# A one-core decode block: the load of w2's blocks 6 to 9 in transfers of 112, 9 and 7 partitions, and the wait for the result's store behind the section

## The chip, the cores and the metric

The kernel runs on one core of a Trainium2 chip. The metric is the device time of one execution in microseconds (us), lower is better. The time before is the median of three runs. A further execution was recorded by the hardware profiler; its rows are what this document reads.

## The reference

One decode step of a transformer layer for four sequences, one token each, in bfloat16: layer norm, attention over a cache of 4096 keys and values for 32 heads, and a dense layer with the activation h * tanh(softplus(h)).

```python
x = A_x                                   # [4, 1, 640]
q = (layernorm(x) @ A_wq)                 # [4, 32 heads, 1, 128]
p = softmax(q . k_cache * 128 ** -0.5)    # k_cache [4, 32, 4096, 128]
h = x + (p @ v_cache) @ A_wo              # v_cache [4, 32, 4096, 128]
u = layernorm(h) @ B_w1 + B_b1            # B_w1 [640, 1728]
h2 = h + (u * tanh(softplus(u))) @ B_w2   # B_w2 [1728, 640]
```

The two caches are 134 MB each; everything is read once.

## The kernel before

**Attention.** The work is cut into 16 units (four groups of eight heads for each of four sequences). A unit's keys or values are one transfer of 128 partitions by 65536 bytes, into one of three slots of SBUF. For a unit VectorE multiplies the keys by the broadcast query in the slot (line 628), TensorE sums over the head dimension with an identity matrix (L640), VectorE reduces (L615), a softmax follows (L677 to L725), and TensorE multiplies with the values (L750). The loads are issued on SP's queue long ahead; a slot is loaded again when its last reader is done.

**The tail.** After the last units the freed slots take the weights of the rest, each with its own transfers, all issued from SP by the helper `load` (its `dma_start` is L867): two halves of wo, three parts of w1, then w2 into slot `wend2`. w2 has 13 whole blocks of 128 rows and a rest of 64 rows, which is loaded alone (L892) into partitions 64 to 127. The boundaries of the transfers of the 13 blocks stand in `W2P`; the first 12 blocks lie two rows to a partition, so that one packet holds 2560 bytes:

```python
W2P = (0, 6, 10, 12, C2)      # C2 = 13: blocks 0-5, 6-9, 10-11, 12
w2_view = B_w2[0 : C2E * 128, :].rearrange("(m p k) n -> p m (k n)", p=128, k=2)
```

The transfer of blocks 6 to 9 is 128 partitions by two packets of 2560 bytes, 640 KB; that of blocks 10 and 11 is 128 by one packet, that of block 12 is 128 by one packet of 1280 bytes, and it is the last load of the kernel.

TensorE then projects with wo (L966), the second layer norm follows (L1007 to L1060), the products with w1 (L1032), the activation on VectorE and ScalarE (L1070 to L1091), and the products with w2 (`w2_products`, L1118). These go in the order of the loads: the rest of 64 rows, then the transfers in order, each group waiting for its transfer's semaphore (w2_0, w2_6, w2_10, w2_12) and for the activation. VectorE and ScalarE copy the four partial rows out of PSUM (`gather`, L1134), and SP stores 4 x 640 values (L1143).

**Who orders it.** The instructions are not scheduled by the framework. A small recorder, the class `Program`, takes every operation with the names that it reads and writes (`P.add`, and `do` for the tail), works out the semaphore waits, and writes each engine's instructions in order, the loop over the units included. A transfer adds 16 to its semaphore when all of it has landed; each transfer has a semaphore named after it. `P.emit()` runs inside `tc.tile_critical()`, one section for the framework, and the section ends with SP's wait for the store's semaphore:

```python
with tc.tile_critical():
    P.emit()
    nc.sync.wait_ge(P.sems["out"], P.totals["out"])
```

Behind the section the framework writes its own closing steps: a handshake of SP with the other engines for the section (the profile gives it the line of the `with`, L1148), and then the closing barrier of the kernel (L1176).

Of the kernel before, what the change touches and what calls it, by code (L numbers as in the profile page):

```python
# [223 lines left out]
def kernel(  # L224
# [13 lines left out]
    nc = tc.nc  # L238

    B, Sq, D = A_x.shape  # L240
# [31 lines left out]
    W2P = (0, 6, 10, 12, C2)  # L272
# [21 lines left out]
    S_BANK, TR, QQ, OB, OT = [("bank", i) for i in range(4)], *[("bank", i) for i in range(4, 8)]  # L294
# [40 lines left out]
    P = Program(nc, tc, 1, NU - 1, NS)  # L335
# [4 lines left out]
    def cells(i, lo=0, hi=SLOT):  # L340

        return [("slot", i, p, k) for p in range(lo // PART, -(-hi // PART)) for k in range(NQ)]
# [5 lines left out]
    def load_kv(what, rows, u, i, parts=1):  # L348
        w = SLOT // parts
        for k in range(parts):  # L350
# [41 lines left out]
            out=ident[:, :],  # L392
# [27 lines left out]
    def bn_stats():  # L420
        for s in range(2):
# [13 lines left out]
            out=ln_std[:, :], in_=ln_mv[:, 1:2], func=ACT.Sqrt, bias=eps_t[0:N, :], scale=1.0  # L435
# [13 lines left out]
            out=ln1_bf,  # L449
# [40 lines left out]
    def identity_sums(dst, pattern, name, **kw):  # L490
# [13 lines left out]
            out=own[:, :], in0=own1[:, :], scalar1=-1.0, scalar2=1e30, op0=ALU.add, op1=ALU.mult  # L504
# [27 lines left out]
    def q_all():  # L532
        for h in range(H):
# [15 lines left out]
            out=qT[:, 0 : NU * G].rearrange("p (o b g) -> p b o g", o=NO, b=N),  # L549
# [273 lines left out]
    def slot_of(u):  # L823
        return 1 if u == 0 else 2 * u % NS
# [21 lines left out]
    i1, i2, i3 = slot_of(NU - 1), slot_of(NU - 2), slot_of(NU - 3)  # L846
# [11 lines left out]
    def load(out_ap, in_ap, i, lo, hi, name, sem=None):  # L858


        ops = {}
        for cell in cells(i, lo, hi):
            for d in P.readers.get(cell, {}).values():
                ops[d.nth] = d
        P.add(
            "SP",
            lambda: nc.sync.dma_start(out=out_ap, in_=in_ap),  # L867
            w=[name],
            sem=sem or "_".join(map(str, name)),
            after=ops.values(),  # L870
        )
# [3 lines left out]
    for k0, k1 in zip(W1P, W1P[1:]):  # L875
# [17 lines left out]
        w=["w2r"],  # L893
        sem=f"slot{i2}",
    )
    for k0, k1 in zip(W2P, W2P[1:]):
        if k0 < C2E:
            assert k0 % 2 == k1 % 2 == 0
            to = wend2[:, k0 * D : k1 * D].rearrange("p (m n) -> p m n", n=2 * D)
            of = w2_view[:, k0 // 2 : k1 // 2]  # L900
        else:
            to, of = w2_sb[:, k0, :], B_w2[k0 * 128 : k1 * 128, :]
        load(to, of, i2, k0 * D, k1 * D, ("w2", k0))

    at = [nw2]

    def scratch(n, dt=FP32):
        a = at[0]
        w = n * (2 if dt == FP32 else 1)
        w += w % 2  # L910
        at[0] = a + w
        ap = wend2[:, a : a + w]
        return ap.bitcast(FP32)[:, 0:n] if dt == FP32 else ap[:, 0:n]

    def do(eng, emit, r=(), w=()):

        return P.add(eng, emit, r=r, w=w, after=[last_pv])
# [123 lines left out]
    for dc in range(DC):  # L1041
        w1 = ("w1", max(k0 for k0 in W1P if k0 <= dc))
        do("PE", lambda dc=dc: h1_pass(dc), [w1, "h2T"], [QQ])
        if dc == 1:
# [4 lines left out]
                    out=std, in_=v_ps, func=ACT.Sqrt, bias=eps_t[:, :], scale=1.0  # L1049
# [22 lines left out]
    def stt(out_, a, scalar, b, op0, op1, r, w):  # L1072
# [13 lines left out]
            out=tc_, in0=tb, scalar1=-0.5, scalar2=-1.0, op0=ALU.mult, op1=ALU.add  # L1086
# [27 lines left out]
    def w2_products(blocks):  # L1114
        for c in blocks:
            w2 = w2_sb[:, c, :] if c < C2 else w2r_sb
            for t in range(OT4):
                ins = nc.tensor.matmul(  # L1118
                    y2[32 * t : 32 * t + N, :],
                    lhsT=act_t[:, c, :],  # L1120
                    rhs=w2[:, t * DT : (t + 1) * DT],
                    start=False,
                    stop=(c == C2 - 1),
                )
        return ins
# [1 line left out]
    do("PE", residual, ["hT", "ident_f"], [S_BANK[1]])  # L1127
    do("PE", lambda: w2_products([C2]), ["w2r", "act"], [S_BANK[1]])
    for k0, k1 in zip(W2P, W2P[1:]):
        do("PE", lambda b=range(k0, k1): w2_products(b), [("w2", k0), "act"], [S_BANK[1]])  # L1130
    out_bf = scratch(D, BF16)[0:N, :]

    def gather(t, copy):
# [11 lines left out]
        sem="out",  # L1145
    )

    with tc.tile_critical():  # L1148
        P.emit()
        nc.sync.wait_ge(P.sems["out"], P.totals["out"])  # L1150


# [28 lines left out]
```

## Time and profile before

| | us |
|---|---|
| median of three runs | 666.3 (666.23 to 666.72) |
| profiled execution, its own time | 666.91 |
| its span, first to last instruction | 665.1 |
| TensorE busy in the span | 378.2 (57%) |
| VectorE busy | 352.4 (53%) |
| ScalarE busy | 89.1 (13%) |
| read from HBM | 283.35 MB, 426 GB/s over the span |
| mean granted TensorE clock | 0.821 |

The profile's page gives busy time by engine, 40 equal slices of the span, the DMA queues (q1 is SP's), the chain of work that ended last, and groups of equal instructions with their source line (L). PE is TensorE's matmul, PEld its weight load, DVE VectorE, ACT ScalarE, POOL GpSimd, SP the sync engine; SPq stands for SP's own instructions, those that issue DMAs among them. Times in the span count from its first instruction. Beside the page the trace was asked for stretches of the span, for single lines, for waits, and read packet by packet at the end of the load.

### The profile page before, as it was taken

What the parts mean: (1) busy time and instruction counts of PE and PEld (TensorE: products, weight loads), DVE (VectorE), ACT (ScalarE), POOL (GpSimd) and SP (SyncE); (2) the same over time, 40 slices, a digit from 0 to 9 for tenths busy, and PEclk for the clock granted to TensorE, in tenths of its full rate; (3) what the DMA queues carried; (4) which work ended last, traced back from release to release, by engine and by line L of the source; (5) the groups of instructions that cost most, each with busy time, mean ns of one, the idle gap of its engine ahead of it and who ended that gap; (6) DMA issues with size and microseconds to landing.
All of it is one profiled execution on the core that took longest, in us unless ns stands there. A gap on an engine that the chain in (4) does not pass through costs nothing.

```text
span 665.1 us, 6908 instructions
## 1 busy us (share of the span) xinstructions
PE 378.2 (57%) x2803; PEld 173.3 (26%) x2803; DVE 352.4 (53%) x313; ACT 89.1 (13%) x318; POOL 2.4 (0%) x12
## 2 busy tenths in 40 slices
PE   0355768375482837548283754828375582837765
PEld 0221323132130313213031322303132230313334
DVE  2065869184472818447390835738093573809402
ACT  0102020202002020200202020020202002020211
POOL 1000000000000000000000000000000000000000
PEclk9999799779596978959697895969788596978865
DMA  9999999999999999999999999999999999999996
GB/s 379 438 441 435 441 388 442 438 437 427 434 434 426 430 437 441 434 430 437 434 422 434 437 441 434 430 434 430 430 430 441 437 430 437 434 430 430 420 417 253
DMA packets 6685, 283.52 MB, mean 426 GB/s; under 512 B 713, under 2 KB 913, under 8 KB 2066
## 3 DMA queue, kind: packets, MB, share of 16 engines
q1 hardware_dynamic: 6664, 283.35, 99.0%
q8 instruction: 8, 0.13, 0.1%
q14 instruction: 3, 0.02, 0.0%
q10 hardware_dynamic: 10, 0.01, 0.0%
HBM read 283.35 MB, written 0.01 MB: 426 GB/s over the span
## 4 chain that ended last, share of the span: by engine, by line
DMA 44%; DVE 25%; PE 19%; another core or an unknown queue 6%; issue 2%; SPq 2%; ACT 1%; DVEq 0%; POOL 0%; ACTq 0%
DMA slot<-in_A_k_cache_dram 41%; DVE slot L628 21%; PE bank L640 13%; PE bank L750 5%; DMA slot<-in_B_w_dram 3%; DVE s_sb L615 3%; SPq L867 2%; ACT e L725 1%; PE bank L708 0%; DVE mx L695 0%; PE bank L686 0%; DVE rl L802 0%; DVE otn L809 0%; DVEq L217 0%
## 5 line engine op out<-in xcount | busy, mean ns | idle before, releaser
L640 PE MATMUL bank<-slot,ident 128*128 128x512 bf16 x1024 | 271.1, 419 | 246.1 <-DVE slot L628 246.1
L628 DVE TENSOR_TENSOR slot<-slot,qb 128x4096 bf16<-128x4096 bf16 x128 | 288.3, 2284 | 156.3 <-DMA slot<-in_A_k_cache_dram 151.9
L640 PEld LDWEIGHTS bank<-slot,ident 128*128 128x128 bf16 x1024 | 100.6, 106 | 401.8 <-DVE slot L628 278.8
L615 DVE TENSOR_REDUCE s_sb<-bank 128x64 f32<-128x512 f32 x64 | 44.0, 688 | 55.7 <-PE bank L640 55.7
L725 ACT ACTIVATE e<-s_sb,nb 128x256 bf16<-128x256 f32 x128 | 63.1, 494 | 46.9 <-DVE nb L717 46.9
L750 PE MATMUL bank<-slot,e 128*32 128x512 bf16 x1024 | 61.2, 393 | 5.2 <-DMA slot<-in_A_v_cache_dram 3.4
L595 ACT CAST qb<-bank 128x128 bf16<-128x128 f32 x17 | 4.5, 265 | 306.1 <-PE bank L586 306.1
L750 PEld LDWEIGHTS bank<-slot,e 128*32 128x32 bf16 x1024 | 26.4, 99 | 38.1 <-issue 8.7
L770 ACT COPY o_sb<-bank 128x512 f32<-128x512 f32 x16 | 9.4, 585 | 183.6 <-PE bank L750 183.6
L695 DVE TENSOR_REDUCE mx<-bank 1x8 f32<-1x128 f32 x16 | 4.5, 279 | 39.9 <-PE bank L686 39.9
L725 ACT ACTIVATION_READ_ACCUMULATOR e<-s_sb,nb 128x1 f32 x128 | 23.9, 187 | 0.0
L783 PE MATMUL bank<-sel,o_sb 128*128 128x8 f32 x136 | 18.5, 262 | 0.0
L783 PEld LDWEIGHTS bank<-sel,o_sb 128*128 128x128 f32 x136 | 17.4, 200 | 0.0
L802 DVE RECIPROCAL rl<-bank 128x8 f32<-128x8 f32 x17 | 3.4, 202 | 15.6 <-PE bank L783 15.6
L535 PE MATMUL bank<-xT,slot 128*128 128x4 bf16 x160 | 4.4, 168 | 10.8 <-DMA slot<-in_A_wq_dram 10.8
L708 PE MATMUL bank<-mx,nscale 1*128 1x8 f32 x32 | 6.1, 262 | 5.9 <-DVE mx L695 5.9
L569 DVE COPY b1T<-bank 128x14 f32<-128x14 f32 x1 | 0.2, 173 | 14.2 <-PE bank L559 14.2
L781 PEld LDWEIGHTS bank<-rs,ones_f 128*128 128x128 f32 x34 | 6.5, 197 | 3.8 <-ACT o_sb L770 1.6
L708 PEld LDWEIGHTS bank<-mx,nscale 1*128 1x128 f32 x32 | 4.7, 183 | 10.6 <-DVE mx L695 10.6
L535 PEld LDWEIGHTS bank<-xT,slot 128*128 128x128 bf16 x160 | 4.3, 104 | 10.9 <-DMA slot<-in_A_wq_dram 10.9
L677 DVE TENSOR_REDUCE pm<-s_sb 128x1 f32<-128x256 f32 x16 | 6.7, 420 | 0.5
L686 PE MATMUL bank<-ident_f,pm 128*1 128x128 f32 x32 | 6.1, 272 | 1.2 <-DVE pm L677 1.2
(75 smaller groups left out, 67.6 us busy)
## 6 DMA issues: line engine op xcount, KB each, us to landing
slot<-in_A_v_cache_dram SPq DMA_DIRECT2D x2, 4096.0 KB, 45.3
slot<-in_A_wq_dram SPq DMA_DIRECT2D x1, 5120.0 KB, 15.3
slot<-in_A_wo_dram SPq DMA_DIRECT2D x2, 2560.0 KB, 33.6
slot<-in_B_w_dram SPq DMA_DIRECT2D x2, 864.0 KB, 34.0
slot<-in_B_w_dram SPq DMA_DIRECT2D x1, 960.0 KB, 31.9
slot<-in_B_w_dram SPq DMA_DIRECT2D x1, 640.0 KB, 32.9
slot<-in_B_w_dram SPq DMA_DIRECT2D x1, 432.0 KB, 33.7
slot<-in_B_w_dram SPq DMA_DIRECT2D x1, 320.0 KB, 22.5
```

Source lines behind the costliest of these rows:

```text
L535: ins = nc.tensor.matmul(qT_ps[:, :, h], lhsT=wq_sb[:, c, h * Dh : (h + 1) * Dh], rhs=xT[:, c, :], start=(c == 0), stop=(c == DC - 1),)
L615: lambda: nc.vector.tensor_reduce(out=s_sb[:, part * RP : (part + 1) * RP], in_=s_bank[part][:, :].rearrange("p (r w) -> p r w", w=W), axi ...
L628: return nc.vector.tensor_tensor(out=kt, in0=kt, in1=qbs[u % NS][:, k * DQ : (k + 1) * DQ] .unsqueeze(1) .to_broadcast([128, RP, DQ]), op= ...
L640: ins = nc.tensor.matmul(s_bank[part][:, :].rearrange("p (r w) -> p r w", w=W), lhsT=ident[:, :], rhs=kt[:, :, d : d + W], start=(d == 0), ...
L677: lambda: nc.vector.tensor_reduce(out=pm[:, :], in_=s_sb[:, :], axis=AX.X, op=ALU.max),
L708: lambda: nc.tensor.matmul(nb_ps, lhsT=nscale[:, :], rhs=mx[:, :], start=True, stop=True),
L725: ins = nc.scalar.activation(out=e2[:, :, h, :], in_=s_sb[:, :].rearrange("p (g r) -> p g r", r=RQ), func=ACT.Exp, bias=nb[:, h : h + 1], ...
L750: ins = nc.tensor.matmul(o_bank[t : t + G * RQ, :], lhsT=e2[:, g, :, :], rhs=vt[:, g * RQ : (g + 1) * RQ, :], start=(g < CT), stop=(g >= N ...
L770: lambda: nc.scalar.copy(out=o_sb[:, :], in_=o_bank[:, :]),
L781: nc.tensor.matmul(l_ps, lhsT=ones_f[:, :], rhs=rss[u % NS][:, :], start=True, stop=True)
L783: ins = nc.tensor.matmul(o_ps, lhsT=o_sb[:, r * Dh : (r + 1) * Dh], rhs=sel[:, r, :], start=(r == 0), stop=(r == RQ - 1),)
L867: lambda: nc.sync.dma_start(out=out_ap, in_=in_ap),
```

## The change

Two edits. First, the load of blocks 6 to 9 is cut by partitions, 0 to 111, 112 to 120 and 121 to 127, into three transfers, issued one after the other; the other w2 transfers stay whole. The three share the semaphore w2_6, and the products of these blocks wait for all of them. Second, SP's wait for the store is taken out of the section and written behind it, with the count in a register and a declared dependence on the section.

```diff
+    w2_parts = {}
     for k0, k1 in zip(W2P, W2P[1:]):
...
-        load(to, of, i2, k0 * D, k1 * D, ("w2", k0))
+
+        cuts = (0, 112, 121, 128) if k0 == W2P[1] else (0, 128)
+        for p0, p1 in zip(cuts, cuts[1:]):
+            load(to[p0:p1], of[p0:p1], i2, k0 * D, k1 * D, ("w2", k0, p0), f"w2_{k0}")
+        w2_parts[k0] = [("w2", k0, p0) for p0 in cuts[:-1]]
...
-        do("PE", lambda b=range(k0, k1): w2_products(b), [("w2", k0), "act"], [S_BANK[1]])
+        do("PE", lambda b=range(k0, k1): w2_products(b), [*w2_parts[k0], "act"], [S_BANK[1]])
...
-    with tc.tile_critical():
+    with tc.tile_critical() as section:
         P.emit()
-        nc.sync.wait_ge(P.sems["out"], P.totals["out"])
+
+    wait = nc.sync.wait_ge(P.sems["out"], nc.sync.to_reg(P.totals["out"]))
+    tc.add_manual_dep(
+        wait.ins,
+        section.name,
+        mybir.DependencyInfo(mybir.DependencyClass.NoSync, mybir.DependencyReason.DATA),
+        reason="the store is issued in the section",
+    )
```

In the built program the engines' other instructions stand in the same order as before; on SP two DMA instructions are added, and its wait for the store stands in the handshake behind the section, after the drain and before the last step.

## The prediction

> **What bounds the kernel now.** I read the page first, then the last microseconds by stretches, then what the last matmuls and SP's last instructions wait for.
>
> From the page: span, DMA slices, and the queues with their packets.
>
> ```profile
> span 665.1 us, 6908 instructions
> ...
> DMA  9999999999999999999999999999999999999996
> ...
> q1 hardware_dynamic: 6664, 283.35, 99.0%
> ...
> q10 hardware_dynamic: 10, 0.01, 0.0%
> ```
>
> The 16 DMA engines are over 90% busy in every slice but the last. 283.35 MB must come in, and only what happens in or after the last slice can end earlier by rearrangement. Both edits lie there. The profiled execution took 666.91 us, 1.79 us more than its span; the median of the runs shown is 666.3, 0.6 below it. I work out differences on the profiled one and take them from the median.
>
> The end of the load, in stretches (columns: stretch, its length, busy time of PE, PEld, DVE, ACT, POOL, granted clock, share of the 16 DMA engines that is busy, GB/s):
>
> ```profile
> 655.00:658.50 3.50, 2.06 (x59) 1.62 (x56) 1.74 (x7) 1.88 (x4) 0.00 (x0) 0.50 1.04 370
> 658.50:659.00 0.50, 0.49 (x18) 0.50 (x21) 0.00 (x0) 0.00 (x0) 0.00 (x0) 0.50 0.94 351
> 659.00:659.50 0.50, 0.50 (x20) 0.27 (x8) 0.00 (x0) 0.00 (x0) 0.00 (x0) 0.50 0.79 284
> 659.50:660.00 0.50, 0.11 (x4) 0.00 (x0) 0.00 (x0) 0.00 (x0) 0.00 (x0) 0.50 0.59 220
> 660.00:660.50 0.50, 0.42 (x16) 0.36 (x16) 0.00 (x0) 0.00 (x0) 0.00 (x0) 0.50 0.28 102
> 660.50:661.00 0.50, 0.38 (x18) 0.09 (x8) 0.00 (x0) 0.00 (x0) 0.00 (x0) 0.50 0.09 31
> 661.00:662.00 1.00, 0.64 (x12) 0.10 (x7) 0.31 (x1) 0.30 (x2) 0.00 (x0) 0.50 0.00 0
> ```
>
> The engines don't finish together: the share falls from 0.94 to 0.09 over two microseconds. The trace's packet records say it exactly: the packets of the last transfer (block 12 of w2) are through on the first engine at 658.87 us and on the last two at 660.81 and 660.82; the next before these is 0.2 us earlier. All engines were given equal bytes, so this is the lag that each carries from earlier, not its share.
>
> From the timeline, the last products, the copies out and the store:
>
> ```profile
> 660.08 1.55 PE L1118 MATMUL bank<-slot 128*4 128x160 bf16 x28 [0.47 <-DMA slot<-in_B_w_dram]
> ...
> 661.33 0.09 PEld L1118 LDWEIGHTS bank<-slot 128*4 128x4 bf16 x4 [0.32 <-DMA slot<-in_B_w_dram]
> 661.69 0.58 ACT L1134 CAST slot<-bank 4x160 bf16<-4x160 f32 x2 [4.59 <-PE bank L1118]
> 661.69 0.65 DVE L1134 CAST slot<-bank 4x160 bf16<-4x160 f32 x2 [3.33 <-PE bank L1118]
> 662.37 0.35 SPq L1143 DMA_DIRECT2D out_dram<-slot  x1
> ```
>
> PE waits for the load at 660.08, 660.91 and 661.33, the last time for w2_12. So the slowest DMA engine sets the end, followed by one chain of products, copies, store and closing steps.
>
> What stands between the store's landing and the span's end (instructions of lines 1148 and 1176; duration min/median/max in ns, first and last start), and SP's wait:
>
> ```profile
> L1148 SPq EVENT_SEMAPHORE  x3: 17/28/28, 663.9 to 664.1; - x3
> L1148 SPq COMPARE_BRANCH  x1: 38/38/38, 663.7 to 663.7; - x1
> L1176 SPq DRAIN  x3: 7/7/7, 664.3 to 664.6; - x3
> SPq L1148 <- DMA out_dram<-slot: 1.0, 1, 1.0
> ```
>
> The store lands at 663.70. Only then does SP run the closing handshake of the section (line 1148: an event, the other engines' drains, two more events and a NOP), and only then the kernel's own closing barrier (line 1176).
>
> **The wait moved behind the section.** It removes the wait from SP's branch and puts it into the handshake. In the built program SP, after issuing the store, branches without waiting, sends its event, drains, and waits in three events: for PE, for DVE and ACT, and third for itself and the store together; then come the NOP and the drains of line 1176. One register move is added, before the wait.
>
> Read singly in the trace of before: wait ends 663.706, event 663.879, drain 663.976, events 664.055 and 664.119, NOP 664.186, line-1176 drains 664.272 and 664.335. After: the third event starts with the landing (663.706 as the branch did), and from there the same steps as before hold: event to NOP 0.067, NOP to drain 0.086, drain to drain 0.063, so the second drain stands at 663.922 instead of 664.335. That is **-0.41 us**. What now hides the earlier handshake is the store's flight: SP's issue ends at 662.72 and the landing is 1.0 us later, while the moved steps (event to second event, 0.24, and the step from branch to event, 0.17) take 0.41, and the register move some 0.05, the step of SP's other small instructions. Without that cover it would cost its 0.41 again. Queued behind the waiting event on SP are only the NOP and the drains; the other four engines have by then passed line 1148 and wait in line 1176's barrier, as before. POOL's closing events, 664.4 to 665.0, follow SP's drain and shift with it.
>
> **Blocks 6 to 9 in three transfers.** Bytes are the same, 640 KB. Two DMA instructions and their semaphore writes are added, nothing else; PE's wait is for 48 instead of 16 on the same semaphore, at 660.08, not the last wait.
>
> SP's side: an issue that finds room takes 0.33 to 0.58 us; two of the last ones are longer:
>
> ```profile
> 627.12 11.17 SPq L867 DMA_DIRECT2D slot<-in_B_w_dram  x1
> 638.33 9.14 SPq L867 DMA_DIRECT2D slot<-in_B_w_dram  x1
> ```
>
> These block because the queue is full, so they end when the DMA engines get on, not after a price of their own. The last load's issue ends at 649.26 and its first packet runs at 658.44 on the fastest engine: 9.2 us of cover. Two issues at 0.58 and up to four more queued packets on an engine, at 0.27 us (the 6912-byte packets running then), come to 1.2 + 1.1 = 2.3 us. I take **0**; the bound above is two more blocked issues (rival below), and nothing is gained, since SP is ahead anyway.
>
> The engines' side: a 128-row transfer gives each engine 8 rows of two 2560-byte packets. The 112 rows give 7 each. For the rest the nearest row is q10: ten packets for a 4-row and a 1-row transfer, that is one data packet per row and one semaphore packet for each of four engines and one engine. So I take one row per engine for the 9 and for the 7. Together engines then carry 7 to 9 rows instead of 8. A row costs 5120 bytes at 370 GB/s / 16, or 0.22 us (2 packets at their median of 0.108 in the trace, the same). So the last engine ends **between -0.22 and +0.24** (a row plus two semaphore packets of about 0.01): down if both late engines get fewer rows, up if either gets one more. The trace doesn't name the engines of its packets, so it can't decide; I take **0** and keep both ends. The engines that end third and earlier leave 0.2 us, so relief cannot exceed about that unless they are relieved too.
>
> [...]
>
> **Sum:** -0.41 + 0 + 0 = -0.41, so 666.3 - 0.4 = **665.9 us**; with the ends of the engines' term 665.7 to 666.1. The three runs of before lie 0.5 us apart. A measurement of this kernel can tell about 0.2% from no change, 1.3 us, so all of this is "within 0.2%".
>
> **Rivals.**
>
> *The short transfers fall on one engine (slower).* 112 is a multiple of 16, but 9 and 7 are odd, and if the splitter finds no share it puts all 16 rows on one engine: 32 packets x 0.108 = 3.5 us there. It decides as soon as that engine is less than 3.5 us ahead of the last, and none is more than 2. From one 2 us ahead: +1.5 - 0.4, 667.4; from one of the last: +3.5 - 0.4, 669.4; from the middle 668.4. Against: q10's four rows were spread one by one. For: no transfer of before has an odd count above one. Chance 0.05, four fifths of it over the bound.
>
> *Rows leave their engine's place (slower).* With 7 rows each, an engine no longer writes the 8 partitions that it writes everywhere else, and engines may get in each other's way where they write. The trace has one 64-row transfer (w2's rest): its 1280-byte packets took a median of 0.060 us, those of the 128-row block 12 took 0.055, and the 2560-byte packets around it (652.6 to 655.65) took 0.139 against 0.107 after. On the most loaded engine 14 + 2 + 2 packets are concerned. If they take 0.139 instead of 0.107: +0.6, on top of its extra row 0.2, less 0.4: 666.7. If all take 0.281, the longest 2560-byte packet of the trace: +3.1, 669.2. From 0.19 a packet on it is slower than before by 1.3 us. Against: the plain 128-row packets beside the 64-row transfer suffered more than its own, so something else than its shape may be the cause. Chance 0.08, a third of it over the bound.
>
> [...]
>
> *SP falls behind.* If each added issue blocks as the two above did, SP is 20.3 us later, less 9.2 of cover: +11, 677; one such block gives about +1.9 - 0.4, 667.8. Chance 0.03.
>
> *The moved wait doesn't do what it says:* if the handshake is still run after the landing, or the register wait costs what it saves, the end stays: 666.3. Chance 0.08, no difference.
>
> *Faster by more.* It needs 1.3 us: 0.4 from the wait, so 0.9 from the engines, though a row is worth 0.22. Only a different lag pattern (two microseconds from first to last engine, all of it from starts and instruction fetches far earlier) could give it: 665.0 or less. Chance 0.07.
>
> **How the numbers follow.** The forecast has 0.69, the unmoved end 0.08, both within 0.2%; two thirds of the 0.08 and a fifth of the 0.05 lie there too: 0.83, less 0.01 for what I don't see, 0.82. Slower: 0.03 + 0.04 + 0.03 + 0.01 = 0.11. Faster: 0.07. The range leaves out most of the faster case and of the slower ones, together under 0.2, and takes in the lower prices of both: 664.9 to 667.4.
>
> **What the next profile would show.** Right: the line of SP's closing branch has no wait; the first event of the section's closing stands before the store's landing; about 0.25 us instead of 0.64 from landing to SP's second closing drain. q1 has 6680 packets, 9 + 7 semaphore packets more; only 2 more would mean one engine each. L1118's last wait ends within 0.25 us of 661.33. [...] A median outside 665.0 to 667.6 would say the sum has missed a term.

## The result: slower, and the profile after

| | before | after |
|---|---|---|
| median (executions) | 666.26 us (8) | 668.18 us (8) |
| lowest to highest | 665.99 to 666.97 | 667.79 to 670.59 |
| profiled execution, its span | 666.91, 665.1 | 669.0, 667.2 |

The ratio is 1.0035 (95% interval 1.0024 to 1.0046), 1.9 us by the medians: outside the predicted range, on the side that had a chance of 0.11. The page of the kernel after has the queue as foretold:

```profile
span 667.2 us, 6911 instructions
...
q1 hardware_dynamic: 6680, 283.35, 99.1%
...
q10 hardware_dynamic: 10, 0.01, 0.0%
```

There are 6680 packets on q1, 16 more than before. That is what one semaphore packet for each of nine and of seven engines gives, so the nine and the seven rows went out one to an engine. The same bytes came. But look at the end of the load, in the same stretches as before (stretch, length, busy time of PE, PEld, DVE, ACT, POOL, granted clock, busy share of the DMA engines, GB/s):

```profile
655.00:658.50 3.50, 1.90 (x45) 1.26 (x42) 1.57 (x6) 1.43 (x3) 0.00 (x0) 0.50 1.13 239
...
659.00:659.50 0.50, 0.00 (x0) 0.00 (x0) 0.00 (x0) 0.00 (x0) 0.00 (x0) 0.50 0.99 189
...
660.50:661.00 0.50, 0.50 (x24) 0.44 (x16) 0.00 (x0) 0.00 (x0) 0.00 (x0) 0.50 1.15 225
661.00:662.00 1.00, 0.28 (x12) 0.00 (x0) 0.00 (x0) 0.00 (x0) 0.00 (x0) 0.50 0.84 159
662.00:663.00 1.00, 0.04 (x4) 0.04 (x8) 0.00 (x0) 0.00 (x0) 0.00 (x0) 0.50 0.52 156
```

Read the last two columns together. The engines are as busy as before (a share of 1, rather more) and bring 239 GB/s instead of 370 in the first stretch. Busy engines that move less mean that each packet takes longer. The packet records say how much: a 2560-byte packet took 0.118 us on the mean of all 768 before and 0.182 after. With 48 such packets to an engine that is 48 x 0.064 = 3.1 us more work for each. From 656 to 658 us, where the last packets of blocks 0 to 5 and the cut ones run side by side, the median was 0.20 to 0.21 us, against 0.107 before. Transfers whose shape was not touched took part: the 1280-byte packets belong to block 12 alone there, which is still one transfer of 128 rows, and from 660 to 662 us, beside the last cut ones, they took medians of 0.106 and 0.110 us instead of 0.055.

From the timeline of the kernel after, the products and the end (start, length, engine, line; the kernel's lines lie 5 later than before):

```profile
660.31 0.97 PE L1123 MATMUL bank<-slot 128*4 128x160 bf16 x24 [1.96 <-DMA slot<-in_B_w_dram]
662.96 1.24 PE L1123 MATMUL bank<-slot 128*4 128x160 bf16 x28 [1.68 <-DMA slot<-in_B_w_dram]
...
663.89 0.09 PEld L1123 LDWEIGHTS bank<-slot 128*4 128x4 bf16 x4 [0.30 <-DMA slot<-in_B_w_dram]
664.25 0.58 ACT L1139 CAST slot<-bank 4x160 bf16<-4x160 f32 x2 [7.61 <-PE bank L1123]
...
664.92 0.30 SPq L1148 DMA_DIRECT2D out_dram<-slot  x1
```

TensorE's last wait for a load ends at 663.89 instead of 661.33: 2.56 us later. The steps from there to the store are as before. The closing steps of the section and of the kernel, and what SP waited for at the end:

```profile
L1153 SPq EVENT_SEMAPHORE  x4: 17/22/509, 665.3 to 665.7; - x4
...
L1188 SPq DRAIN  x3: 7/7/7, 666.4 to 666.7; - x3
```

```profile
SPq L1153 <- DMA out_dram<-slot: 0.5, 1, 0.5
```

The handshake starts at 665.3, before the store has landed, and its third event takes the wait: 0.5 us, until about 666.24. From there to the second closing drain, at 666.43, it takes 0.19 us (0.64 before). So 2.56 - 0.4 is the 2.1 us by which the profiled executions differ: the moved wait gave what was forecast, and the load took six times as much back. One execution differs from the next by up to a microsecond here: with the wait moved alone (the first experiment), the unchanged load ended TensorE's last wait at 660.32 in the profiled execution. By the medians the load took 1.9 + 0.4 = 2.3 us back.

### The profile page after: what moved, and what is told of

It reads as the page before. It is cut to its first block, busy times and chain, and to the rows that moved or that the text cites. A ratio compares the mean times of both kernels' runs of the same rounds, so it can differ in the third digit from the quotient of the medians.

```text
span 667.2 us, 6911 instructions
## 1 busy us (share of the span) xinstructions
PE 379.5 (57%) x2803; PEld 172.6 (26%) x2803; DVE 352.4 (53%) x313; ACT 89.1 (13%) x318; POOL 2.4 (0%) x12
## 3 DMA queue, kind: packets, MB, share of 16 engines
q1 hardware_dynamic: 6680, 283.35, 99.1%
## 4 chain that ended last, share of the span: by engine, by line
DMA 43%; DVE 25%; PE 19%; another core or an unknown queue 6%; SPq 3%; issue 2%; ACT 1%; DVEq 0%; POOL 0%; ACTq 0%
DMA slot<-in_A_k_cache_dram 41%; DVE slot L628 21%; PE bank L640 13%; PE bank L750 5%; SPq L867 3%; DVE s_sb L615 3%; DMA slot<-in_B_w_dram 2%; ACT e L725 1%; PE bank L708 0%; DVE mx L695 0%; PE bank L686 0%; DVE rl L802 0%; PE bank L1123 0%; DVE otn L809 0%
## 5 line engine op out<-in xcount | busy, mean ns | idle before, releaser
L535 PE MATMUL bank<-xT,slot 128*128 128x4 bf16 x160 | 4.4, 168 | 10.6 <-DMA slot<-in_A_wq_dram 10.6
L708 PEld LDWEIGHTS bank<-mx,nscale 1*128 1x128 f32 x32 | 4.7, 182 | 10.6 <-DVE mx L695 10.6
```

The source lines that it names most:

```text
L535: ins = nc.tensor.matmul(qT_ps[:, :, h], lhsT=wq_sb[:, c, h * Dh : (h + 1) * Dh], rhs=xT[:, c, :], start=(c == 0), stop=(c == DC - 1),)
L708: lambda: nc.tensor.matmul(nb_ps, lhsT=nscale[:, :], rhs=mx[:, :], start=True, stop=True),
```

## The experiments

Theory A after this reading: where an engine's rows lie decides, beside those of its neighbours. Rows that don't lie as in a plain transfer of 128 make the DMA engines get in each other's way where they write, and everything beside them is slowed. Its rivals: B, a few engines have extra rows; C, the number of transfers costs; and later D, the collision is in the reads from memory.

### The wait moved alone

```diff
-    with tc.tile_critical():
+    with tc.tile_critical() as section:
         P.emit()
-        nc.sync.wait_ge(P.sems["out"], P.totals["out"])
+    wait = nc.sync.wait_ge(P.sems["out"], nc.sync.to_reg(P.totals["out"]))
...
```

> The wait for the store behind the section, the load of blocks 6 to 9 whole as before. Every theory of the slow load leaves this alone: the sum of the prediction, -0.41 us, 665.9, and 0.25 us instead of 0.64 from the store's landing to SP's second closing drain. If the moved wait costs something instead (a register wait, a longer closing), the time is 666.3 or more.

Measured: 665.86 us against 666.21, ratio 0.9996 (0.9987 to 1.0005). That is -0.35 by the medians, of the forecast size and too small to be told from no change. Its stretch, with the DMA share down to 0.76 because the load is nearly done:

```profile
656.00:660.00 4.00, 2.33 (x61) 1.32 (x53) 1.13 (x4) 0.25 (x1) 0.00 (x0) 0.50 0.76 282
```

### The three transfers alone

```diff
+        cuts = (0, 112, 121, 128) if k0 == W2P[1] else (0, 128)
+        for p0, p1 in zip(cuts, cuts[1:]):
+            load(to[p0:p1], of[p0:p1], i2, k0 * D, k1 * D, ("w2", k0, p0), f"w2_{k0}")
```

> The load of blocks 6 to 9 in 112, 9 and 7 partitions, the wait inside the section as before. If the two edits add up and the load alone is the loss: 666.3 + 1.9 + 0.4 = 668.6. If the loss comes from both together or from the wait: 666.3 to 667.

Measured: 669.38 us, ratio 1.0049 (1.0035 to 1.0063), mean 2560-byte packet 0.174 us. The loss is in this part. It is 3.2 us by the medians, 0.8 more than the 668.6 that the two edits should add up to; these are five executions, from 668.57 to 670.24, and the excess isn't explained.

```profile
656.00:660.00 4.00, 1.23 (x33) 0.70 (x32) 1.38 (x6) 0.29 (x2) 0.00 (x0) 0.50 1.08 202
```

### 112 and 16 partitions

```diff
-        cuts = (0, 112, 121, 128) if k0 == W2P[1] else (0, 128)
+        cuts = (0, 112, 128) if k0 == W2P[1] else (0, 128)
```

> Two transfers, 112 and 16 partitions, the wait as before. Theory A (place): with 7 rows to an engine instead of 8 the engines leave the partitions that each writes in a 128-row transfer and get in each other's way; then most of the loss is here too, +1.5 to +2.5 us, and 2560-byte packets take about 0.2 us from 656 us on. Theory B (few engines): the odd short transfers that use 9 and 7 engines are the cause; 16 rows use all engines once, so the time is that of before within 0.3 us and packets take 0.107. Theory C (count): each added transfer costs by itself; one added instead of two, about +1.1 us.

Measured: 668.72 us, ratio 1.0046 (1.0032 to 1.0060), mean packet 0.165 us. Here every engine has its eight rows again, seven and one (so the packet records have it for this cut of the first K load, below), and the time is not told apart from that with three transfers: the intervals overlap. B falls.

```profile
656.00:660.00 4.00, 1.52 (x35) 0.75 (x28) 1.13 (x4) 0.18 (x1) 0.00 (x0) 0.50 1.06 213
```

### Three transfers of all 128 partitions

```diff
+            parts = [(to[:, 0:1], of[:, 0:1])]
+            parts += [(to[:, 1:2, c : c + D], of[:, 1:2, c : c + D]) for c in (0, D)]
```

> Three transfers again, but each of all 128 partitions: the first 2560 bytes of a row, then two of 1280 bytes; the wait as before. A: before's time within 0.3 us, packets as before (0.107 and 0.055). B: the same as before. C: +2.3 us as with 112, 9 and 7.

Measured: 666.46 us, ratio 1.0008 (0.9995 to 1.0021), packets at medians of 0.107 us for 2560 bytes from 656 us on and 0.055 for 1280 (mean of all 2560-byte ones 0.117, before 0.118). Three transfers, and no loss that can be told from none: C falls.

```profile
656.00:660.00 4.00, 2.21 (x52) 1.21 (x45) 1.13 (x4) 0.25 (x1) 0.00 (x0) 0.50 0.84 302
```

### Two halves, and the even and odd partitions

These are two runs with the same two transfers of 64 rows, the same packets and the same shares. They differ only in which rows go together.

```diff
+        cuts = (0, 64, 128) if k0 == W2P[1] else (0, 128)
```

> Blocks 6 to 9 of w2 in two transfers of 64 partitions, the wait for the store as before. Every engine carries the same 8 rows as with 128, and both counts are multiples of 16, so that no engine has more to do. Theory A (place): 2560-byte packets at 0.15 to 0.25 us instead of 0.107, the last load 1.5 to 3 us later, 667.8 to 669.3, slower by 0.2 to 0.45%. If only shares that are not even (112 and 16 rows give 7 and 1) cost, or only counts of rows below 64: 0.107, and 666.2, the same.

```diff
+        parts = ((0, 127, 2), (1, 128, 2)) if k0 == W2P[1] else ((0, 128, 1),)
+        for p0, p1, ps in parts:
+            load(to[p0:p1:ps], of[p0:p1:ps], i2, k0 * D, k1 * D, ("w2", k0, p0), f"w2_{k0}")
```

> Blocks 6 to 9 of w2 in two transfers of 64 rows as in the run with two halves, but the even partitions and then the odd ones; the wait for the store as before. Same count of transfers, rows, bytes and packets as the halves. Theory A (place: the even partitions lie all over SBUF, the halves on one side of it): 2560-byte packets at 0.107 to 0.12, last load as before, 666.2 (665.9 to 666.7), the same. Theory of the row count (any transfer under 128 rows is slow): packets at 0.17 to 0.2 and 668.3 to 668.6, as the halves. The trial on K had the even and odd rows at 0.614 us for 16 KB packets once the halves before them were through, so A is likelier.

Measured: the halves 668.48 us, ratio 1.0033 (1.0021 to 1.0044), mean packet 0.159 us; the even and odd partitions 666.43 us, ratio 0.9999 (0.9989 to 1.0009), mean packet 0.115 us. The same stretch, first of the kernel before, then of the halves, then of the even and odd partitions:

```profile
656.00:660.00 4.00, 2.34 (x62) 1.66 (x59) 1.56 (x6) 0.90 (x3) 0.00 (x0) 0.50 0.94 354
```

```profile
656.00:660.00 4.00, 1.28 (x37) 0.74 (x31) 1.27 (x5) 0.25 (x1) 0.00 (x0) 0.50 1.06 230
```

```profile
656.00:660.00 4.00, 2.73 (x72) 2.31 (x74) 1.74 (x7) 2.00 (x4) 0.00 (x0) 0.50 0.89 331
```

At a share near 1 the halves bring 230 GB/s, while the even and odd rows, at 0.89, bring 331. (The profiled execution of the even and odd partitions was a late one, 668.31 us against their median of 666.43, so here the rates and packets are compared, not the ends.) So it is neither the cut nor the row count, but the place.

### The cost by itself, on the first K load

The tail has short packets and four shapes at once. The first K load has 16 KB packets and nothing else beside it, so it was cut into four column quarters, each with another cut of the partitions:

```diff
-    load_kv("K", k_rows, 0, 1)
+    SHAPES = (
+        ((0, 128, 1),),
+        ((0, 112, 1), (112, 128, 1)),
+        ((0, 64, 1), (64, 128, 1)),
+        ((0, 127, 2), (1, 128, 2)),
+    )
...
```

> The first K load (128 rows of 64 KB, packets of 16 KB) comes in four column quarters of 2 MB, each in another cut of the 128 partitions: whole; 112 and 16; 64 and 64; the even and the odd partitions. Bytes and packet lengths in memory are the same in all four. At the full rate a 16 KB packet takes about 0.60 us (434 GB/s over 16 engines). Theory A (which rows an engine writes; rows that are not the 8 neighbours of the plain layout make engines get in each other's way at the SBUF side): 0.6 in the first quarter; over 0.75 in the second (up by what the 2560-byte packets showed, 0.165 against 0.107); 0.9 to 1.2 in the third, where only half of the partitions are written at a time; less than the third in the fourth, where the same number of rows is spread over all partitions. Theory D (the reads from memory collide, not the writes): third and fourth alike, since both read 64 rows of 16 KB at a time, from addresses a fixed stride apart. If only short packets suffer, all four stay at 0.6. Span: up by the excess, 8 packets an engine and quarter times it, 1 to 8 us.

Stretches inside the four quarters, in this order (the first begins while the load ahead of it still ends, hence its share of 0.88):

```profile
14.00:19.00 5.00, 2.85 (x106) 2.85 (x107) 0.00 (x0) 0.00 (x0) 0.00 (x0) 1.00 0.88 375
21.00:27.00 6.00, 3.38 (x11) 1.25 (x10) 4.67 (x3) 2.23 (x5) 0.00 (x0) 1.00 1.04 251
29.00:38.00 9.00, 5.12 (x16) 1.76 (x15) 5.09 (x3) 0.00 (x0) 0.00 (x0) 0.70 0.98 206
41.00:44.00 3.00, 0.11 (x1) 0.12 (x2) 2.46 (x2) 0.00 (x0) 0.00 (x0) 0.79 1.01 421
```

And the packets of one engine, in ns, from the packet records (the records don't name the engine; these follow one another because each starts within 4 ns of where the one ahead ended; a bar is the end of a transfer):

```
whole    611 611 611 611 611 611 611 611 |
112, 16  754 1018 1061 1044 1058 832 1087 | 1313 |
halves   2068 1180 1289 1292 | 1116 1208 1291 1292 |
even/odd 1161 806 672 621 | 612 613 621 614 |
```

A whole transfer takes 0.611 us a packet, 112 rows about 1.05, the halves 1.29, and the even and odd rows 0.614. The 16 rows, of which every engine has one, took from 1.02 to 2.33 on the 16 engines, 1.46 at the median. The first even rows are still slow while other engines are still in the halves: the damage is done to whoever runs beside. The execution took 676.85 us, 10.6 more than the median before: more than the 8 expected at most. The halves were above their 0.9 to 1.2; the order of the four is the one that A gave.

What sets these sizes is not shown. Against the 0.611 us of the whole transfer the halves took 2.1 times as long, the 16 rows 2.4 times at the median and 3.8 times at the slowest, and the 112 rows 1.7 times, though they lie all over SBUF but for 16 partitions.

### Written place against read place

The even rows are also read from other addresses than a half. So the two were crossed: quarter two is written to the even and odd partitions and read from the halves, quarter four the other way round.

```diff
+    WHOLE, SPREAD, HALVES = ((0, 128, 1),), ((0, 127, 2), (1, 128, 2)), ((0, 64, 1), (64, 128, 1))
+    SHAPES = ((WHOLE, WHOLE), (SPREAD, HALVES), (WHOLE, WHOLE), (HALVES, SPREAD))
```

> The first K load in four column quarters again: whole; written to the even and then the odd partitions but read from the first and then the second 64 rows; whole; written to the first and then the second 64 partitions but read from the even and then the odd rows. In the second and fourth quarter the rows of the first 128 positions are so permuted in K and not in V, which changes what is computed and not the work. Theory A (the place in SBUF that is written decides): 0.61 us a 16 KB packet in the first three quarters, 1.2 to 1.3 in the fourth; span up by about 5 us (8 packets x 0.65). Theory D (the rows read decide): 1.2 to 1.3 in the second, 0.61 in the fourth; the same total. Both: 1.2 in both, 10 us.

Stretches inside the four quarters:

```profile
15.00:19.00 4.00, 2.73 (x102) 2.73 (x103) 0.00 (x0) 0.00 (x0) 0.00 (x0) 1.00 0.97 418
20.00:23.00 3.00, 1.74 (x43) 1.27 (x40) 1.16 (x2) 1.45 (x6) 0.00 (x0) 1.00 1.02 426
25.00:28.00 3.00, 3.00 (x8) 1.06 (x7) 2.68 (x2) 0.00 (x0) 0.00 (x0) 1.00 1.01 431
32.00:38.00 6.00, 3.96 (x17) 1.40 (x16) 5.61 (x4) 0.00 (x0) 0.00 (x0) 1.00 1.04 218
```

Only the quarter that writes half of the partitions at a time falls to 218 GB/s; its packets took 1.05 to 1.34 us, most of them over 1.2, those of the other three nearly all 0.611. The span grew by 6.3 us, to 671.4, where about 5 were expected. What is written where decides, and D falls.

### The 64-row rest that was there before

The kernel before has one transfer of this kind, the 64-row rest of w2. Two runs take it away: one leaves the load out, one keeps its content and loads 128 rows (with the wait moved).

```diff
-        lambda: nc.sync.dma_start(out=w2r_sb[OVER:128, :], in_=B_w2[FM:F, :]),
```

> The kernel before without the transfer of w2's 64-row rest: that load is left out, its rows stay zero, the products with them run as before. It brings 160 KB less, 0.38 us at 426 GB/s. Theory A (that transfer of 64 rows already slows what runs beside it in the kernel before): from 652 to 656 us the 2560-byte packets fall from 0.128 to 0.142 to about 0.107, and 3456-byte ones from 0.159 to 0.202 to 0.135; time down by 0.4 to 1.2 us. Otherwise (something else in that stretch slows them, the shorter packets or the products' reads): packets stay at 0.128 to 0.142, time down by 0.2 to 0.4 us.

```diff
-        lambda: nc.sync.dma_start(out=w2r_sb[OVER:128, :], in_=B_w2[FM:F, :]),
+        lambda: nc.sync.dma_start(out=w2r_sb, in_=B_w2[F - 128 : F, :]),
...
+    P.add("POOL", lambda: nc.gpsimd.memset(w2r_sb[0:OVER, :], 0.0), w=["w2r"])
```

> The wait moved as in the change, blocks 6 to 9 whole as before, and w2's 64-row rest loaded as 128 rows (the 64 rows ahead of it come too, and GpSimd sets their partitions to zero behind the load, where it did so ahead of it). 160 KB more, 0.38 us at 426 GB/s; the moved wait gives 0.35 to 0.41. Theory A: the packets from 652 to 656 us fall to 0.107 and 0.135, worth 0.4 to 1.2 us: 664.7 to 665.9, the fastest kernel so far by a little. Otherwise 666.2, the same.

The four microseconds around the rest: before, without the rest, with 128 rows.

```profile
652.00:656.00 4.00, 2.97 (x72) 2.74 (x70) 1.17 (x7) 1.10 (x2) 0.00 (x0) 0.50 1.03 332
```

```profile
652.00:656.00 4.00, 3.55 (x95) 3.12 (x95) 1.40 (x8) 1.89 (x4) 0.00 (x0) 0.50 1.03 399
```

```profile
652.00:656.00 4.00, 3.64 (x96) 3.25 (x95) 1.28 (x8) 1.89 (x4) 0.62 (x1) 0.50 1.03 394
```

At the same share of 1.03 the rate goes from 332 to 399 and 394 GB/s; the other runs that keep the 64-row rest have 327 to 350 in this stretch. The 2560-byte packets from 653 us on go from medians of 0.128 to 0.142 us to 0.104 to 0.107 in both. Without the rest the time is 665.79, ratio 0.9990 (0.9982 to 0.9999); 0.19 us of the 0.49 are the bytes left out (80 KB at 426 GB/s; the expectations put them at twice that), so the time alone could not have shown it. With 128 rows and the wait moved it is 665.42, ratio 0.9987 (0.9976 to 0.9998): the fastest of these kernels, below both before and after. It was not run beside the kernel with the wait alone, and their intervals overlap, so how much of its 0.9 us is the wait's and how much the rest's is not settled.

## Why the prediction was wrong, point by point

**The wait, -0.41: right.** The steps moved ahead of the landing as worked out; 0.64 us became 0.19, and the run with this part alone gave -0.35, which its times alone can't tell from none.

**SP's two extra issues, 0: right.** Its last load issue ended at 649.97 instead of 649.26, and the first packets of that load ran from 660.2. That an issue blocks on a full queue agrees with the packet records of before: SP's load issues that began with at most 949 unfinished packets on the queue took up to 0.57 us; the last three began with 1342, 1429 and 1359 and took 11.17, 9.14 and 1.75.

**One row per engine for the 9 and the 7: right**, as far as the 6680 packets tell, and, as the run with 112 and 16 shows, of no account.

**The engines' term, "I take 0", between -0.22 and +0.24: the step that failed.** It counted rows and multiplied them by a duration measured on transfers of 128 rows. Which rows an engine has also changes how long a packet takes, its own and those beside it: 0.182 us instead of 0.118 on the mean of an engine's 48 packets, 3.1 us of work. The last load wait came 2.56 us later, and by the medians the term was +2.3 us, not 0.

**The rival "rows leave their engine's place" was the case, and had 0.08.** The prediction had the last load wait within 0.25 us of 661.33 if it was right; it came at 663.89. The rival's scale was right: "from 0.19 a packet on it is slower than before by 1.3 us", and 0.20 to 0.21 was reached. That its sum at 0.205, 18 x 0.098 + 0.2 - 0.4 = 1.6 us, comes near the measured 1.9 is partly luck, since it let only 14 + 2 + 2 packets suffer and the others suffered too. Its likelier price, with those at 0.139, was too low. What misled me was the argument against it: that the packets beside the 64-row transfer suffered more than its own, "so something else than its shape may be the cause". The runs without the rest and with 128 rows show that its shape was the cause. That neighbours are hurt is how this effect looks, and no sign against it. I had the neighbours' 0.139 against 0.107 in hand, and set it aside; I had not looked at the rate of that stretch alone, 332 GB/s at a busy share of 1.03.

Not settled: how the loss divides between the 112, the 9 and the 7 rows, why the 112 rows are slow (about 1.05 us a packet on K instead of 0.611) though they lie all over SBUF but for 16 partitions, which partitions an engine writes (no record names the engine), and why the rest's own short packets before (at most 0.069 us in any microsecond, instead of 0.055) suffered less than the longer ones beside them.

## What to carry to other kernels

Cut a load along the free dimension (the bytes within a partition), or into the even and the odd partitions, rather than into contiguous groups of partitions: three transfers of 128 rows and two of even and odd rows cost nothing that could be measured (ratios 1.0008 and 0.9999), two halves cost 2.2 us on 640 KB. In a profile the sign is a stretch where the DMA engines are fully busy and the GB/s fall (here 192 to 230 GB/s at 1.06 to 1.08 instead of 354 at 0.94, 656 to 660 us); look then for a transfer of fewer than 128 partitions there, also when the slowed packets are not its own. A duration per packet is only good for the shape on which it was measured: 0.107 us became 0.20 to 0.21 here.

## What the hardware showed that I had not expected

- A 64-row transfer of 80 KB lowered the rate of four microseconds of other transfers from 399 to 332 GB/s (327 to 350 over the runs that have it).
- The damage is mutual, and on K it went on behind the short transfer while other engines were still in it: behind the halves the first even rows took 1.16, 0.81 and 0.67 us before they came down to 0.61.
- The engines are at different transfers at the same time. In the profiled execution before, the first and the last of them are 1.3 us apart in the load at 15 us, 1.9 at 46 us, and 2.2 from about 105 us to the end of the K and V loads near 600. Single instruction fetches (16 KB, 0.95 to 1.10 us each) fall in the stretch where the lag grows, at 22, 54 and 92 us, but those at 122 and 156 us did not widen it. The prediction put all of it down to starts and instruction fetches; what makes it is not shown. In these loads it was not made up.
